# A fused Sinkhorn-attention and Fourier-mixing kernel: W1 loaded by quarters of its columns, and every engine's order and buffers laid out anew

## The chip, the cores and the metric

The kernel runs on one NeuronCore of one Trainium2 chip. A core has five engines that work at the same time: TensorE (PE in the profile, with its weight loads as PEld), VectorE (DVE), ScalarE (ACT), GpSimd (POOL) and SyncE (SP). POOL and SP issue nearly all the DMA transfers. The metric is device microseconds of one execution, from plain runs; the profile is of one more execution, with the hardware profiler on.

## The reference

`_attn_ref` takes q, k and v of shape (4, 8, 768, 64) and an 8 by 8 matrix for each of the 32 pairs of batch and head. Five rounds of exponential and of row and column normalisation (Sinkhorn) turn each matrix into a mixing matrix P. P mixes the eight blocks of 96 rows of k and v, and then each block of q attends to the mixed block of k and v of its own index.

```
k_sorted = np.einsum('bhij,bhjcd->bhicd', P, k_b)      # v_sorted alike
scores = scale * q_b @ k_sb^T;  attn = softmax(scores);  out = attn @ v_sb
```

`_moe_ref` takes the result as x of shape (4, 768, 512), adds the real part of a two-dimensional Fourier transform over tokens and features, normalises each row, and applies an MLP with W1 (512 by 2048) and W2 (2048 by 512).

```
u = x + real(fft2(x));  un = (u - mean) / sqrt(var + 1e-6)
out = u + np.maximum(un @ w_ch1, 0.0) @ w_ch2
```

## The kernel before

The work is cut by batch (b = 0 to 3) and, in the MLP, by half a batch of 384 tokens (g = 0, 1). A batch goes through the following stages. The numbers are operation numbers, which the order tables below use; they are the same before and after.

- Sinkhorn on all 32 matrices at once (VectorE and ScalarE; only for the first batch's start), then the block mixing matrices.
- `v_mix`, `v_mix_two`: v is mixed by TensorE (tag `vmix`, `vmix2`), and evacuated from PSUM (tag `vev`).
- `kqt` and `scores`: k is mixed and q transposed on TensorE (tags `kq`, `qT`, and in batches 1 to 3 `kq4`, `qT4`, which use quarters of the array and 24 small matmuls each), evacuated (`ksev`, `qtev`), multiplied (`sc`, `sc4`), exponentiated on ScalarE (`exp`, line 1270) and written as exp minus one (`em1`, lines 1283 and 1285).
- `av`: attention times v, 13 small matmuls for a head (line 1300), then a reciprocal and a product on VectorE.
- `a_path`, `a_rows`, `dft1`, `dft2`: the Fourier transform as matmuls. Operations 218 and 219 (`psx`, `psr`, lines 1062 and 1072) make the rows of the block means, which SP copies into `rb` (tag `arow`). The first matmul group of `dft1` of batch 0 is operation 244 (line 1374), its first `dft2` is 259 (line 1465). Then come mean and variance, the normalised rows `un`, and the transposed tiles `ut`. In batch 0 TensorE transposes and three evacuations write `ut` (operations 277, 281 and 285, tag `utev`).
- `ff1` (line 1584) for batch 0: for each of 16 column chunks `fc` of W1, four matmuls of 128 by 384 over the four 128-row chunks of W1, then a relu into `hr`. `ff2` (line 1668) multiplies with W2. Batches 1 to 3 use a scheme with seven products in place of eight (`ff1_seven`, line 1764, and `ff2_chunk`, lines 1864 and 1874), with sums and differences of the quarters of W1 and W2 (`w1_sums`, `w2_sums`).

The order of the work is not the order of the program text. Every operation is registered with `P.add`, with its possible engines, its durations and its dependences. The table `ORDER` holds, for each engine, the list of operation numbers in which that engine's instructions are written out. `Plan.schedule` goes through these lists with assumed durations. Its result sets three things in the emitted program: which buffer (PSUM bank, SBUF tile) each operation gets, the interleaving of the instructions, and how many idle matmuls (line 2010, "spins", on a constant tile) are written into TensorE's stream ahead of the operation 1613, `spun`. It does not write any wait; waits follow from the data and the buffers.

The assumed durations in `Plan` that matter here: a load moves at `HBM` = 390 bytes per ns of source data and lands `DLAT` us after that; `FETCH` = (190, 255, a, b) says that TensorE's instructions come in blocks of 256, that the block after next is asked for 190 instructions in, and that it takes a us while loads are running and b us otherwise.

Loads are issued by POOL (line 616, `load`) in the order of its list. Operations 28 to 31 load W1, 430 and 431 the second half of v, 432 to 435 load W2, 117 to 122 k and q of batch 1, 474 to 485 those of batch 2, 667 to 678 those of batch 3. All loads of large inputs cast from 32 to 16 bits on the way. POOL and SP keep eight semaphores each for their transfers; a further transfer reuses the semaphore of the eighth before it.

Of the kernel before, what the change touches and what calls it, by code (L numbers as in the profile page):

```python
# [12 lines left out]
ALU = mybir.AluOpType  # L13
# [17 lines left out]
FETCH = (190, 255, 6.0, 3.5)  # L31
# [36 lines left out]
    ),  # L68
    "ACT": (
# [27 lines left out]
    ),  # L97
    "DVE": (
# [183 lines left out]

class Plan:
    HBM = 390.0
    DLAT = 2.2
    XL = 0.07

    def __init__(self):
# [52 lines left out]
    def schedule(self):  # L341
# [56 lines left out]
        while len(order) < len(self.ops):  # L398
            pick = None
            for e in free:  # L400
                if place[e] == len(queue[e]):
                    continue
                o = queue[e][place[e]]
# [1639 lines left out]
```

## Time and profile before

| | us |
|---|---|
| plain runs: median of 3 (lowest, highest) | 258.41 (257.62, 258.8) |
| profiled execution, its own time | 256.77 |
| profiled execution, span from first to last instruction | 255.0 |
| TensorE busy in the span | 241.3 |
| VectorE busy | 225.0 |
| ScalarE busy | 178.0 |
| GpSimd busy | 95.3 |

The profile has a page with the busy time of each engine and the span in 40 slices, and views that answer questions on the same execution: the chain of work that ended last (each step follows back to what released it), the busy time of each engine in chosen stretches, instructions in order of time, groups of instructions by line and tile, and the DMA transfers. In the view of stretches a cell such as "5.31 (x103)" is the busy time in us and the number of instructions. A matmul is counted from its start to a modelled end, so neighbours overlap; a run of matmuls is read by its total time and its count.

### The profile page before, as it was taken

Reading aid. Unit: us, or ns where it says so; the run is one execution under the profiler, and the core shown is the slowest. Engines: PE = TensorE matmul, PEld = TensorE weight load, DVE = VectorE, ACT = ScalarE, POOL = GpSimd, SP = SyncE. Lnnn points to the kernel's source line nnn. Section 1 sums busy time; section 2 is a strip of 40 time slices with the busy share of each in tenths; the row PEclk is TensorE's granted clock in tenths of the full one; section 3 lists DMA queues with packets and bytes.
Section 4 is the critical chain, followed back from the end, with each engine's and each line's share of the span. In section 5 each row is a group of like instructions: output and inputs, shape, how many; then the busy total and the mean of one; then the engine's idle time right before and its main releaser. Section 6 shows DMA issues by size and latency. Waiting matters only on the chain.

```text
span 255.0 us, 7508 instructions
## 1 busy us (share of the span) xinstructions
PE 241.3 (95%) x2975; PEld 163.3 (64%) x2975; DVE 225.0 (88%) x576; ACT 178.0 (70%) x418; POOL 95.3 (37%) x128
## 2 busy tenths in 40 slices
PE   4989989999999999999999999999999999999990
PEld 1356865566666566655556667887667887658880
DVE  4789898899999899989999999998999688799870
ACT  2589898999998999999858898244784523664100
POOL 8975522243708950216446000061240007530070
PEclk9999999999999999999999999999999999999999
DMA  6999999999999998482685123652466304880055
GB/s 128 206 213 305 212 212 217 208 218 248 195 117 123 152 154 138 131 150 53 93 179 114 35 75 63 85 88 38 84 75 71 62 4 63 121 107 0 3 108 139
DMA packets 45688, 31.77 MB, mean 125 GB/s; under 512 B 30554, under 2 KB 39528, under 8 KB 45652
## 3 DMA queue, kind: packets, MB, share of 16 engines
q0 software_dynamic: 26544, 23.59, 59.2%
q1 hardware_dynamic: 19110, 7.72, 16.8%
q8 instruction: 23, 0.38, 0.6%
q14 instruction: 11, 0.09, 0.1%
HBM read 29.07 MB, written 11.53 MB: 159 GB/s over the span
## 4 chain that ended last, share of the span: by engine, by line
PE 80%; ACT 10%; DMA 3%; DVE 3%; issue 2%; ACTq 0%; POOLq 0%
PE bank L1764 22%; PE bank L1864 12%; PE bank L1874 9%; PE bank L1668 9%; PE bank L1584 6%; PE bank L1300 4%; DMA hr<-in_v_dram 3%; PE bank L1261 3%; ACT ks L859 2%; PE bank L1465 2%; ACT ex L1270 2%; PE bank L1374 2%; PE bank L1072 1%; PE bank L877 1%; ACT eb L1285 1%
## 5 line engine op out<-in xcount | busy, mean ns | idle before, releaser
L1612 POOL DMA_INDIRECT out_dram<-u,rows x23 | 37.9, 1646 | 109.9 <-DVE u L1892 66.4
L1270 ACT ACTIVATE ex<-bank 96x384 f32<-96x384 f32 x64 | 29.4, 487 | 2.9 <-PE bank L1261 2.5
L1864 PEld LDWEIGHTS <-hr 128*128 128x128 f16 x288 | 28.0, 98 | 5.1 <-DVE hr L1839 0.4
L1764 PE MATMUL bank<-ut,w1sb 128*128 128x384 f16 x144 | 30.9, 326 | 0.0
L859 ACT COPY bank<-bank 128x384 f32<-128x384 f32 (+1 forms) x42 | 18.6, 445 | 13.8 <-DVE hr L1784 4.9
L1764 PEld LDWEIGHTS <-w1sb 128*128 128x128 f16 x192 | 18.6, 98 | 11.1 <-issue 0.2
L1787 ACT ACTIVATE hr<-bank 128x384 f16<-128x384 f32 x41 | 19.1, 492 | 9.2 <-PE bank L1764 8.7
L1584 PE MATMUL bank<-ut,w1sb 128*128 128x384 f16 x128 | 24.5, 326 | 0.0
L1668 PE MATMUL bank<-w2sb,hr 128*128 128x512 f16 x96 | 24.4, 380 | 0.0
L1874 PEld LDWEIGHTS <-vcx 128*128 128x128 f16 x216 | 21.1, 98 | 3.6
L616 POOL DMA_DIRECT2D kq<-in_q_dram x18 | 16.6, 931 | 7.8 <-PE bank L877 3.7
L1764 PEld LDWEIGHTS <-kq 128*128 128x128 f16 x144 | 13.9, 98 | 8.8 <-issue 0.2
L1300 PEld LDWEIGHTS <-eb 97*128 97x128 f16 x416 | 16.3, 98 | 3.8 <-issue 0.2
L1874 PE MATMUL bank<-kq,vcx 128*128 128x256 f16 x144 | 18.5, 273 | 0.0
L1285 ACT ACTIVATE eb<-ex 96x384 f16<-96x384 f32 x37 | 18.3, 521 | 0.1
L1864 PE MATMUL bank<-w2sb,hr 128*128 128x256 f16 x144 | 17.8, 273 | 0.0
L1772 DVE TENSOR_TENSOR hr<-bank,vsf 128x384 f16<-128x384 f32 x32 | 16.8, 550 | 1.2 <-PE bank L1764 1.0
L1300 PE MATMUL bank<-vsf,eb 97*128 97x65 f16 x416 | 17.4, 193 | 0.2
L1317 DVE TENSOR_TENSOR rt<-bank,rz 128x384 f16<-128x384 f32 x32 | 16.9, 545 | 0.3
L859 DVE COPY bank<-bank 128x384 f32<-128x384 f32 (+1 forms) x24 | 12.1, 508 | 5.3 <-PE bank L1874 3.7
L859 ACT CAST vsf<-bank 96x512 f16<-96x512 f32 x25 | 15.7, 676 | 0.5 <-PE bank L976 0.4
L859 ACT CAST ks<-bank 128x384 f16<-128x384 f32 x29 | 15.1, 559 | 0.9 <-PE bank L1195 0.8
(212 smaller groups left out, 587.2 us busy)
## 6 DMA issues: line engine op xcount, KB each, us to landing
w1sb<-in_moe_w_ch_dram POOLq DMA_DIRECT2D x4, 512.0 KB, 18.0
w2sb<-in_moe_w_ch_dram POOLq DMA_DIRECT2D x4, 512.0 KB, 22.2
hr<-in_v_dram POOLq DMA_DIRECT2D x2, 768.0 KB, 9.2
kq<-in_v_dram POOLq DMA_DIRECT2D x2, 768.0 KB, 12.4
kq<-in_k_dram POOLq DMA_DIRECT2D x8, 192.0 KB, 5.5
kq<-in_q_dram POOLq DMA_DIRECT2D x16, 96.0 KB, 7.2
out_dram<-u SPq DMA_DIRECT2D x6, 256.0 KB, 2.2
out_dram<-u POOLq DMA_DIRECT2D x5, 256.0 KB, 4.6
```

The costliest lines, as they stand in the source:

```text
L859: (nc.scalar.copy if e == "ACT" else V.tensor_copy)(dst, src)
L1270: nc.scalar.activation(ex.ap[0:96], pss[h2].ap[0:96, 0:384], AF.Exp, scale=SCALE),
L1285: nc.scalar.activation(ed, src, AF.Identity, bias=-1.0)
L1300: nc.tensor.matmul(po.ap[:, 65 * T:65 * T + 65], eb.ap[:, e0:e0 + 128], vsf[0:97, vi:vi + 65], start=(n == 0), stop=(n == len(WIN[T]) - 1) ...
L1317: P.add({"DVE": (0.465, 0.56)}, lambda _: V.tensor_tensor(rt.ap[:, :, D * h:D * h + D], po3()[:, :, 0:D], rz.ap[:, :, None].broadcast_to([ ...
L1584: nc.tensor.matmul(ps.ap[:, 0:GT], w1sb[:, c, 128 * fc:128 * fc + 128], ut.ap[:, c, :], start=(c == 0), stop=(c == 3))
L1612: return nc.gpsimd.indirect_dma_start(out.rearrange("b s m -> (b s) m"), bass.IndirectOffsetOnAxis(ap=rows[:, i:i + 1], axis=0), t_, None, ...
L1668: nc.tensor.matmul(ps.ap, hr[g][:, fc, 128 * tt:128 * tt + 128], w2sb[:, fc, :], start=(fc == 0), stop=(fc == 15))
L1764: nc.tensor.matmul(ps.ap[:, 0:GT], lhs[:, c, fi], rhs()[:, c, :], start=(start and c == 0), stop=(c == 1), skip_group_check=True)
L1787: nc.scalar.activation(hr[g][:, fc, :], p.ap[:, 0:GT], AF.Relu)
L1864: nc.tensor.matmul(ps.ap[:, 0:256], lhs[:, fc], rhs[:, fc], start=(start and fc == 0), stop=(fc == 7), skip_group_check=True)
L1874: nc.tensor.matmul(ps.ap[:, 0:256], S.ap[:, fc], rhs[:, fc], start=False, stop=(fc == 7), skip_group_check=True)
```

## The change

- `load_w1(c)` loads columns 512c to 512c + 511 of all four row chunks, where it loaded all 2048 columns of row chunk c. Each of the four transfers moves the same number of bytes, in runs of 2 KB of source where they were 8 KB.
- `ff1` for chunk `fc` now depends on the one quarter `fc // 4`, where it depended on all four loads. The keys in `w1_sums` follow.
- `FETCH` becomes (190, 255, 7.0, 4.0), where it was 6.0 and 3.5. `DLAT` becomes 2.9, where it was 2.2. `Plan.schedule` also holds a transfer of POOL or SP back until the eighth transfer before it on that engine has landed.
- All five lists of `ORDER` are new. No operation is added or removed. 141 operations change from ScalarE to VectorE or the other way.

The core of the diff; of `ORDER` only the first rows of the three lists that the text speaks of most:

```diff
-FETCH = (190, 255, 6.0, 3.5)
+MOVES = ("load", "out", "acc", "uX", "qX", "arow")
+FETCH = (190, 255, 7.0, 4.0)
...
     "PE": (
-        "0 77 69 78 73 79 91 123 139 92 141 125 211 97 127 143 218 129 134 "
-        "105 115 109 107 101 113 103 175 145 111 155 219 150 187 171 159 173 "
-        "157 190 177 196 182 193 161 166 208 332 318 335 205 199 320 328 202 "
-        "330 389 341 322 357 324 244 326 248 250 255 257 338 354 259 263 267 "
-        "344 287 436 292 437 360 349 438 297 276 280 284 402 370 365 932 1613 "
-        "940 563 930 918 386 928 942 373 408 920 916 411 938 922 405 914 926 "
+        "0 77 69 91 73 78 92 79 139 123 141 125 211 127 143 97 218 129 113 "
+        "107 115 134 101 103 145 105 111 109 150 171 219 159 173 175 187 318 "
+        "190 177 193 182 155 157 196 161 166 205 357 208 320 202 328 199 341 "
+        "332 326 324 389 335 330 244 322 248 250 257 255 354 338 259 263 267 "
+        "360 287 292 436 344 437 349 438 276 297 365 280 284 402 1613 934 942 "
+        "928 920 373 370 916 924 932 408 914 563 386 376 918 411 922 405 926 "
...
     "POOL": (
-        "18 19 20 21 5 6 7 1 2 3 4 10 8 22 23 24 25 26 27 334 117 118 119 120 "
-        "121 122 430 431 28 29 30 31 432 433 434 435 474 475 476 477 478 479 "
-        "314 480 481 482 483 484 485 667 668 669 670 671 672 310 951 673 674 "
+        "18 19 20 21 5 6 7 1 2 3 4 10 8 22 23 24 25 26 27 334 118 30 122 119 "
+        "431 117 430 432 31 121 29 28 120 310 433 434 474 476 477 475 435 479 "
+        "478 482 483 485 480 670 678 484 481 314 669 668 671 672 667 957 677 "
...
     "SP": (
-        "12 13 14 15 17 16 232 231 230 233 428 426 275 283 429 427 279 590 "
+        "12 13 14 15 230 233 231 232 17 16 283 427 426 275 279 428 429 590 "
...
-    DLAT = 2.2
+    DLAT = 2.9
...
+        lane = {"POOL": [0.0] * 8, "SP": [0.0] * 8}
...
                 t = max(free[e], o.ready, st)
+                if e in lane and o.tag in MOVES:
+                    t = max(t, lane[e][0])
...
+            if e in lane and o.tag in MOVES:
+                lane[e] = lane[e][1:] + [o.end]
...
     def load_w1(c, prio):
-        load(w1sb[:, c, :], w1v[:, c, :], 1048576, [("w1", c)], prio)
+        f = slice(512 * c, 512 * c + 512)
+        load(w1sb[:, :, f], w1v[:, :, f], 1048576, [("w1", c)], prio)
...
             P.add(pe(mm(GT, 4)), f, r=[(ut, tt, 1) for tt in range(3)]
-                  + [("w1", c) for c in range(4)], w=[ps], prio=pr_pe,
-                  tag="ff1")
+                  + [("w1", fc // 4)], w=[ps], prio=pr_pe, tag="ff1")
...
-                (G3, X11, G3, ALU.subtract, w1k, [("w1", 0), ("w1", 1)]),
+                (G3, X11, G3, ALU.subtract, w1k, [("w1", 2), ("w1", 3)]),
```

190 rows, old and new, of the table ORDER are left out of this document.

## The prediction

> **What bounds the kernel now.** I read the page's slices first, to find where which engine is full, and then the view of stretches.
>
> ```profile
> span 255.0 us, 7508 instructions
> ...
> PE   4989989999999999999999999999999999999990
> ...
> DVE  4789898899999899989999999998999688799870
> ACT  2589898999998999999858898244784523664100
> ...
> ```
>
> ```profile
> 3.76:14.47 10.71, 10.25 (x37) 3.91 (x37) 8.18 (x33) 5.26 (x7) 10.71 (x14) 1.00 1.10 201
> 14.47:26.48 12.01, 10.35 (x187) 7.49 (x188) 11.41 (x30) 11.14 (x25) 6.74 (x12) 1.00 1.22 263
> 26.48:32.62 6.14, 6.07 (x132) 4.63 (x130) 5.14 (x17) 5.43 (x15) 3.35 (x6) 1.00 1.29 213
> 32.62:38.62 6.00, 4.73 (x133) 3.84 (x131) 5.79 (x18) 5.52 (x13) 1.49 (x2) 1.00 1.03 213
> 38.62:44.49 5.87, 5.76 (x129) 3.39 (x130) 4.92 (x12) 4.97 (x12) 1.36 (x2) 1.00 1.07 217
> 44.49:53.53 9.04, 9.04 (x176) 5.71 (x164) 8.24 (x25) 8.98 (x24) 2.82 (x4) 1.00 1.14 207
> 53.53:249.50 195.97, 195.14 (x2216) 134.34 (x2209) 180.27 (x441) 135.14 (x324) 66.17 (x84) 1.00 0.69 100
> ```
>
> The columns after the length are PE, PEld, DVE, ACT, POOL, the granted clock, the DMA share and GB/s. I chose the last boundary, 53.53, because the first `ff1` matmul starts there. Behind it TensorE is idle for 195.97 - 195.14 = 0.83 us in all. Busy is not yet dense, so I also looked at the chain of waits, whose longest pieces behind that point are runs of matmuls:
>
> ```profile
> 37.40 1.22 issue
> ...
> 53.00 0.47 ACT ut L859
> ...
> 185.07 8.48 PE bank L1764 x52
> ...
> 219.09 11.20 PE bank L1764 x68
> ...
> 249.07 0.42 DVE eb L1892
> ```
>
> 52 matmuls in 8.48 us are 163 ns each, 68 in 11.20 are 165: one pace, with no gaps in it. So I take the last 196 us to hold nothing to win but those 0.83 us. The end is set by when the first `ff1` can start, plus TensorE's work that is left then, plus the tail behind 249.5, whose operations stand in the same order in the new lists. The first `ff1` waited for the last transposed tile, which ScalarE wrote from 53.00 to 53.47.
>
> The second thing to see is the stop of 1.22 us at 37.40, where TensorE waited for nothing that the profile shows. Two more rows explain it:
>
> ```profile
> q8 instruction: 23, 0.38, 0.6%
> ...
> 81.51:87.24 5.73, 5.73 (x133) 1.00 1.23 140
> 87.26:94.39 7.13, 6.89 (x148) 1.00 1.65 144
> ```
>
> 23 packets of 0.38 MB are 16.5 KB each, and 2975 matmuls with 2975 weight loads over 23 are 259 instructions each: these are blocks of TensorE's instructions. The three stretches 26.48 to 32.62, 32.62 to 38.62 and 38.62 to 44.49 hold about 128 matmuls each, one block, and took 6.14, 6.00 and 5.87 us, though the middle one holds only 4.73 us of work. While the loads run, a block costs about 6 us, and TensorE stops if its work in a block is less.
>
> The Trainium skill ("Runtime: NRT & Kernel Launch", Instruction fetch mechanics) says that a block of 256 instructions is fetched ahead and that the cost of a boundary is "mostly hidden". This trace disagrees at one boundary of 23, with 1.22 us.
>
> **The change, part by part.** All sums are made against the profiled execution (span 255.0, own time 256.77); I carry the difference over to the median of the plain runs, 258.41, which lies 1.64 us above it.
>
> *W1 by quarters of its columns.*
>
> ```profile
> L1584 PE MATMUL bank<-ut,w1sb x128: 323/326/337, 53.5 to 110.5; 128*128 128x384 f16 x128
> ...
> L616 POOL DMA_DIRECT2D w1sb<-in_moe_w_ch_dram x4: 528/528/528, 27.0 to 30.5; - x4
> ...
> DMA to landing us min/median/max: 17.7/18.0/19.8
> ```
>
> ```profile
> L616 POOL DMA_DIRECT2D w2sb<-in_moe_w_ch_dram x4: 740/744/750, 31.3 to 40.9; - x4
> ```
>
> W1 lands by 30.5 + 19.8 = 50.3, and its first use is at 53.5: today no `ff1` waits for it. A quarter of columns has the shape of a W2 load (2 KB runs, 512 of them), so POOL spends 0.74 us instead of 0.53 on each, 0.84 us in all, hidden because POOL runs far ahead of its landings. The new list puts quarter 0 (operation 28) behind 5440 KB of loads counted from operation 118 and including itself, by the sizes in the code after the cast; today's last W1 load closes 5120 KB.
>
> ```profile
> cs<-k_cs POOLq DMA_DIRECT2D x1, 579.0 KB, 8.4
> tab<-k_tab POOLq DMA_DIRECT2D x1, 514.0 KB, 10.2
> perm<-k_perm POOLq DMA_DIRECT2D x1, 34.0 KB, 10.1
> ...
> 15.36 0.56 POOL L616 DMA_DIRECT2D tab<-k_tab  x1
> 15.89 0.56 POOL L616 DMA_DIRECT2D perm<-k_perm  x1
> ```
>
> `perm`, the load before, lands at 15.89 + 10.1 = 26.0. From there 5120 KB took 24.3 us, so 5440 take 25.8, and quarter 0 lands near 51.8. The first four `ff1` of the new list (934, 942, 928, 920) use quarters 2, 3, 1 and 0, so that the split matters for 2 us at most; 920 comes some 2 us behind the first. Cost 0, with 3 to 4 us to spare.
>
> *TensorE's list ahead of the first `ff1`.* `psr` (219) cannot start before the table `tab` lands at 15.36 + 10.2 = 25.6, and nothing ahead of that load moved. By counting matmuls in both lists, 374 instructions stand ahead of `psr` (382 before), and 1034 ahead of the first `dft1` (1034 before). With 6 us per block the first `dft1` can hardly come earlier than its 40.5. What can go is the time that the other engines lost around the stop:
>
> ```profile
> 37.91 0.26 ACT L1347 COPY pmt<-pmt 128x4 f16<-128x4 f16 x1
> 39.05 0.86 ACT L859 COPY qt<-bank 128x384 f16<-128x384 f16 x2 [0.88 <-PE bank L1139]
> ```
>
> ScalarE idles for 0.88 us, waiting for q transposes behind the stop. In the new list the transposes 357 and 341 both stand ahead of the block's end, with evacuations of 0.43 us each for ScalarE to do. I take -0.9, with bounds of -1.3 (the 0.41 us idle before the next `dft1` evacuation too) and 0.
>
> *Operations that change engine.* Ahead of the last transposed tile, ScalarE gains 20 operations and loses 21, and VectorE gains 20 and loses 19. I priced them by these groups and their like:
>
> ```profile
> L859 ACT CAST vsf<-bank 96x512 f16<-96x512 f32 x13 | 8.2, 676 | 0.0
> ...
> L1285 ACT ACTIVATE eb<-ex 96x384 f16<-96x384 f32 x7 | 3.6, 521 | 0.0
> ```
>
> ```profile
> L1283 DVE TENSOR_SCALAR eb<-ex 96x384 f16<-96x384 f32 x13 | 4.3, 349 | 0.2
> ...
> L859 DVE CAST vsf<-bank 96x512 f16<-96x512 f32 x3 | 2.1, 684 | 0.0
> ```
>
> For instance six v evacuations go to VectorE (6 x 0.68) and seven `em1` leave it (7 x 0.35). All together ScalarE is relieved of 0.4 us and VectorE loaded with 1.4. ScalarE was the later one, so -0.4. VectorE had 6.14 - 5.14 = 1.0 us idle from 26.48 and 5.87 - 4.92 = 0.95 from 38.62, which covers 1.4; if it covers nothing, the first `ff1` comes 1.0 us later. I take 0.
>
> *Behind the first `ff1`.* Operation 370 (`kq4`) falls behind it, in the dense part: +0.4. Changes between array shapes number 82 instead of 81, at about 0.1 each by
>
> ```profile
> 111.30 0.97 PE bank L1668 x4
> ...
> 113.94 0.86 PE bank L1668 x4
> ```
>
> (the first follows a group of small matmuls): +0.1. Of the 0.83 us idle I give back 0.2.
>
> *Moved steps on SP and POOL.* SP's small loads 17 and 16 now stand behind four copies of block-mean rows. They are used by the store 310 and by the first `dft2`, behind 44.49, and should have some microseconds to spare, since operations that sum to about 3 us stand behind VectorE's `rr` in the new list that stood ahead of it. On POOL the store 310 stands ahead of W2's later loads, and waits for VectorE:
>
> ```profile
> 50.27 0.16 DVE L1500 SCALAR_TENSOR_TENSOR u<-rt,bank 128x2 f32<-128x2 f16 x1
> ```
>
> ```profile
> L1668 PE MATMUL bank<-w2sb,hr x96: 377/379/390, 67.6 to 133.7; 128*128 128x512 f16 x96
> ```
>
> The loads queued behind it are issued from about 52, when transfers until 52.7 are still ahead of them (5632 KB from 26.0), and W2 is first read at 67.6. Both at 0; if the loads starved, `ff2` would wait for what they are late.
>
> The sum: -0.9 - 0.4 + 0.4 + 0.1 - 0.2 = **-1.0 us**: 255.8 profiled, 257.4 in plain runs.
>
> **The rivals.**
>
> *The dense part gets stops (slower).* Instruction blocks behind 53.5 are not all as roomy as today's, where the tightest that I measured took 5.73 us with 5.73 of work. Adding up starts in the new list, one block between operations 450 and 596 (four `vmix2`, `kq4`, `sc4`, little `ff2`) holds only about 4.3 to 4.7 us, and one between 976 and 519 about 4.8 to 5.2. If a block costs 6 us there as between 26 and 44, this adds 1.5 + 1.0 = 2.5 us of TensorE's time, with VectorE's extra microsecond 3.5; less the gains of 1.0, +1.5 to +2.5, so 260.4. For it: the row 87.26 to 94.39 has a DMA share of 1.65, more than any of the early blocks. Against: no block behind 53.5 shows a stop today. It decides from a block time of about 5 us on.
>
> *Nothing moves.* The list of what TensorE does ahead of the first `ff1` is the same but for 370, the first `dft1` stays at its place by the block count, and VectorE's 1.4 us eat ScalarE's gap: 258.4. W1 by quarters would then also show as what it is in the rows, a load that nobody waited for.
>
> *The early stop vanishes.* If the 1.22 us are not the price of a block, the new order may be free of them, the first `dft1` comes up to 1.0 earlier, and the sum is -2.0. Also, plain runs lie 1.64 us above the profiled one; if that is late loads and stops that vary from run to run, an order that leaves more room for them gets some of it back. With half of the second that makes -2.8, 255.6. The Trainium skill's "mostly hidden" (same page and section) points to this one; the row at 37.40 is against it.
>
> *The new order is tight where the old one is loose.* DVE and ACT are full up to 130 us (the slices show nines), so a swap there can hold up TensorE at once. No row shows the new swaps; I count it with the first rival.
>
> **How the numbers follow.** Main case 0.42 (257.4, own range 256.4 to 258.4), nothing moves 0.20 (257.9 to 258.9), dense stops 0.23 (259.2 to 261), early stop gone 0.15 (255 to 256.6). A measurement of this kernel tells about 0.5%, 1.3 us, from no change, so the bounds are 257.1 and 259.7. Faster: 0.15 and not quite half of 0.42, 0.35. Slower: 0.23 and a little of the rest's tail, 0.25. Same: 0.40. The range goes from 255.5 to 260.7, through most of the two outer cases.
>
> **What would show it.** Right: first `ff1` at 52.3 to 53; ScalarE's idle time behind the stop under 0.3 us; the first `dft1` within 0.5 us of 40.5; TensorE idle under 1 us behind the first `ff1`; no wait of `ff1` for `w1sb`. Wrong: "issue" pieces over 0.5 us behind 70 us (dense stops); a first `ff1` that waits for VectorE's `ut` after 54 (VectorE overloaded); a wait of line 1584 for a W1 load (the list too late); a first `dft1` before 39.8 (no block price).

## The result, and the profile after

| | before | after |
|---|---|---|
| median of 20 plain runs, us (lowest, highest) | 257.96 (256.99, 259.61) | 259.59 (257.69, 262.23) |
| ratio, 95% interval | | 1.0056 (1.0032 to 1.008) |
| profiled execution, span, us | 255.0 | 256.5 |

The ratio leaves out three executions of the changed kernel that were over 261.5 us, more than 1.5% above its fastest, so it lies a little under the quotient of the two medians.

The changed kernel came out 0.56% slower, where the forecast was 0.4% faster (257.4 against 258.41). Four repeats of the changed kernel, told below, gave 0.9943, 0.9964, 0.9980 and once more 1.0035 of before. So there are two results to explain.

The page of the changed kernel, to be laid beside the page of before:

```profile
span 256.5 us, 7512 instructions
...
PE 243.4 (95%) x2982; PEld 164.8 (64%) x2982; DVE 227.3 (89%) x575; ACT 178.6 (70%) x419; POOL 93.5 (36%) x128
...
PE   4799999999999999899999999999999999999992
...
PE 77%; DVE 10%; DMA 4%; ACT 4%; issue 2%; POOL 1%; DVEq 0%; SPq 0%; POOLq 0%
```

TensorE's two early 8s, at the third and the sixth slice, are gone, though the second slice fell from 9 to 7 (there are 34 spins in place of 27). There is a new 8 at the 17th slice, from 102.6 to 109.0 us, where before had a 9. The view of stretches, with the same boundaries as for before, and the last one from the first `ff1` on:

```profile
32.62:38.62 6.00, 5.74 (x147) 3.94 (x145) 5.78 (x19) 5.15 (x14) 1.57 (x3) 1.00 1.07 211
...
44.49:53.53 9.04, 8.84 (x141) 5.14 (x134) 8.46 (x25) 8.45 (x23) 3.50 (x5) 1.00 1.18 217
54.23:252.00 197.77, 195.58 (x2233) 135.45 (x2233) 180.33 (x438) 135.29 (x326) 65.90 (x85) 1.00 0.67 98
```

In the stretch of the old stop TensorE is now busy for 5.74 us, not 4.73; but 1.21 us of it are spins, and before had none there. And the first `ff1` starts at 54.23, 0.70 us later than before, and behind it TensorE is idle for 197.77 - 195.58 = 2.19 us, where it was 0.83. The span divides so: first `ff1` +0.70; from there to the last matmul's end 197.75 us against 195.51, +2.24; from there to the end of the span 4.54 against 5.96, -1.42. The sum is +1.52, the difference of the spans. None of the three is what was forecast.

**Where TensorE stops.** Instructions in order of time around 102 us in the changed kernel (start, duration, engine, line; in brackets the idle time before and what ended it):

```profile
100.00 1.35 POOL L1618 DMA_INDIRECT out_dram<-u,rows  x1 [6.63 <-DVE mv L1527]
...
101.66 1.01 POOL L1618 DMA_INDIRECT out_dram<-u,rows  x1 [0.19 <-issue]
...
102.32 0.59 ACT L866 CAST ks<-bank 128x384 f16<-128x384 f32 x1 [1.27 <-PE bank L1591]
...
103.26 0.20 DVE L1321 RECIPROCAL rz<-bank 128x6 f32<-128x6 f32 x1 [1.09 <-PE bank L1307]
...
103.51 0.60 ACT L866 CAST ks<-bank 128x384 f16<-128x384 f32 x1
...
104.16 0.36 PE L1268 MATMUL bank<-qt,ks 64*64 64x96 f16 x16 [1.07 <-ACT ks L866]
```

TensorE waits for ScalarE's `ks`, and ScalarE had stood idle for 1.27 us itself, waiting for TensorE. It needed op 680 (`kq4`), whose matmuls by their rows ended at 100.6. VectorE likewise waits for an `av` (op 655) that by its rows ended at 102.44, and starts at 103.26. The trace also records when TensorE raised its semaphore, the counter that the other engines' instructions wait for. For the matmuls that end at 100.41, 100.59, 101.39, 102.04 and 102.44 by the rows it went up at 101.33, 102.29, 103.04, 103.10 and 103.24: 0.8 to 1.7 us late, where the usual lag is 0.01. ScalarE's copy starts 0.03 us behind the second of these raises and VectorE's reciprocal 0.02 us behind the last. So the results were announced late, one by one and then bunched, while the rows go on at their pace. All five ends lie between 100.00 and 102.67, when GpSimd issued two indirect stores (stores whose target rows come from a table); the last raises came up to 0.57 us behind the second. The profile has three more such places, each at a score (line 1268) that ends inside an indirect store: 0.81 us late at 50.54, 1.22 at 109.08, 0.49 at 126.0. The profile of before shows 0.28 at most. Besides, the trace of the changed kernel lacks eight of TensorE's raises, most of them for results that end inside an indirect store; the trace of before lacks none.

The Trainium skill ("Perfetto Trace Analysis", Tensor Engine Instruction (MATMUL, LD_WEIGHTS)) says that a matmul's end is estimated from its size, and that the semaphore goes up only when PSUM has acknowledged all bytes. That is why such a delay is in no matmul row; the trace agrees, with 101.39 in the row and 103.04 at the semaphore.

### The profile page after: what moved, and what is told of

Same layout as the page of the kernel before. It is cut to its first block, busy times and chain, and to the rows that moved or that the text cites. A ratio compares the mean times of both kernels' runs of the same rounds, so it can differ in the third digit from the quotient of the medians.

```text
span 256.5 us, 7512 instructions
## 1 busy us (share of the span) xinstructions
PE 243.4 (95%) x2982; PEld 164.8 (64%) x2982; DVE 227.3 (89%) x575; ACT 178.6 (70%) x419; POOL 93.5 (36%) x128
## 3 DMA queue, kind: packets, MB, share of 16 engines
q0 software_dynamic: 28080, 23.59, 59.6%
## 4 chain that ended last, share of the span: by engine, by line
PE 77%; DVE 10%; DMA 4%; ACT 4%; issue 2%; POOL 1%; DVEq 0%; SPq 0%; POOLq 0%
PE bank L1770 19%; PE bank L1591 8%; PE bank L1674 8%; PE bank L1870 8%; PE bank L1307 5%; PE bank L1880 5%; PE bank L1268 4%; PE bank L1381 3%; PE bank L1472 3%; DMA out_dram<-u,rows 2%; PE bank L884 2%; DVE vcx L1845 2%; PE bank L955 2%; DVE hr L1778 1%; PE bank L2016 1%
## 5 line engine op out<-in xcount | busy, mean ns | idle before, releaser
L1618 POOL DMA_INDIRECT out_dram<-u,rows x23 | 36.8, 1601 | 82.5 <-DVE u L1898 37.3
L866 ACT COPY bank<-bank 128x384 f32<-128x384 f32 (+1 forms) x52 | 22.5, 443 | 12.0 <-PE bank L1880 9.6
L1770 PEld LDWEIGHTS <-w1sb 128*128 128x128 f16 x192 | 18.7, 98 | 11.8 <-issue 0.2
L1793 ACT ACTIVATE hr<-bank 128x384 f16<-128x384 f32 x36 | 16.8, 492 | 9.8 <-PE bank L1770 9.3
L1292 ACT ACTIVATE eb<-ex 96x384 f16<-96x384 f32 x43 | 22.4, 528 | 0.4
L622 POOL DMA_DIRECT2D kq<-in_q_dram x18 | 15.6, 878 | 12.9 <-DVE rz L1321 7.3
L1591 PEld LDWEIGHTS <-w1sb 128*128 128x128 f16 x128 | 11.1, 97 | 6.8 <-issue 0.4
L1602 ACT ACTIVATE hr<-bank 128x384 f16<-128x384 f32 x31 | 14.8, 496 | 0.9 <-PE bank L1591 0.7
L866 ACT CAST ks<-bank 128x384 f16<-128x384 f32 x25 | 13.7, 575 | 1.5 <-PE bank L1591 1.3
## 6 DMA issues: line engine op xcount, KB each, us to landing
out_dram<-u SPq DMA_DIRECT2D x6, 256.0 KB, 2.3
out_dram<-u POOLq DMA_DIRECT2D x4, 256.0 KB, 6.7
```

What stands on the lines that cost most here:

```text
L866: (nc.scalar.copy if e == "ACT" else V.tensor_copy)(dst, src)
L1292: nc.scalar.activation(ed, src, AF.Identity, bias=-1.0)
L1591: nc.tensor.matmul(ps.ap[:, 0:GT], w1sb[:, c, 128 * fc:128 * fc + 128], ut.ap[:, c, :], start=(c == 0), stop=(c == 3))
L1618: return nc.gpsimd.indirect_dma_start(out.rearrange("b s m -> (b s) m"), bass.IndirectOffsetOnAxis(ap=rows[:, i:i + 1], axis=0), t_, None, ...
L1770: nc.tensor.matmul(ps.ap[:, 0:GT], lhs[:, c, fi], rhs()[:, c, :], start=(start and c == 0), stop=(c == 1), skip_group_check=True)
```

## The experiments

Ratios are to the kernel before on the same chip, with 95% intervals. Runs of one section without another word shared a chip.

### One part at a time

`old_quarters` takes from the change only the W1 part:

```
-        load(w1sb[:, c, :], w1v[:, c, :], 1048576, [("w1", c)], prio)
+        f = slice(512 * c, 512 * c + 512)
+        load(w1sb[:, :, f], w1v[:, :, f], 1048576, [("w1", c)], prio)
...
```

> The kernel before with one part of the change alone: W1 loaded by quarters of its columns, and ff1 and the sums of W1 waiting for their quarter; the order and the planner's delays are those of before. Theory (the order is what costs): 258.0, within 0.5 of before, first ff1 near 53.5 in the profile, because the W1 quarters land ahead of it as the row chunks did. Rival (quarters cost): 259.5, with ff1 waiting for W1 or loads landing later. Rival (quarters help and the order hides it): 257.0 or less.

Measured: 256.0 us, 0.9941 (0.9919 to 0.9963). The second rival: quarters help. Later, on another chip, `old_quarters2` gave 0.9945. But nothing moved up to the last matmul, which started at 248.90 against 248.76. The gain is at the very end (see the drain below).

`old_delays` takes only `FETCH`, `DLAT` and the lanes:

```
-FETCH = (190, 255, 6.0, 3.5)
+FETCH = (190, 255, 7.0, 4.0)
...
-    DLAT = 2.2
+    DLAT = 2.9
...
```

> The kernel before with the planner's delays and lanes of the change alone (7.0 and 4.0 us per block fetch, 2.9 us landing, eight lanes per queue); order and W1 chunks are those of before, so that only the choice of buffers and the count of spins differ. Theory (the order costs): 258.0, within 0.5 of before. Rival (the buffers laid out under the new delays cost, through waits for a buffer that was free before): 259.5, with waits in the dense part. Rival (more spins push the first blocks): first dft1 later than 40.8 and 258.6.

Measured: 257.82 us, 1.0004 (0.9975 to 1.0034): no effect, as the theory said.

`new_olddelays` is the changed kernel with these lines taken back:

> The changed kernel with the planner's old delays and no lanes: order and W1 quarters of the change, buffers and spins laid out as before. Theory (the order costs): 259.6, as the change, first ff1 near 54.2. Rival (buffers cost): 258.0.

Measured: 256.7 us, 0.9962 (0.9941 to 0.9983). This is below both expectations. The theory that the order costs 0.56% falls: with quarters the order loses some 0.2% against `old_quarters` (256.7 against 256.0), and the two intervals overlap.

`new_rows` is the changed kernel with the W1 part taken back:

> The changed kernel with W1 loaded by chunks of its rows again; order and delays are those of the change. Theory (the order costs): 259.6, as the change. Rival (quarters cost): 258.0. Rival (quarters are needed under the new order, since its first ff1 uses two quarters only): over 260, with the first ff1 waiting for the last W1 load.

Measured: 258.14 us, 1.0025 (1.0 to 1.005). The number is that of the first rival, "quarters cost", but not its reason, since `old_quarters` had gained. There was no wait for W1: the first `ff1` started at 53.43.

None of these four profiles had a TensorE result over 0.35 us late, though in the two with the new order the same scores end inside the same stores (the one near 50 us 0.51 and 0.52 us behind the store's start, as in the first profile). From 0.9962 and 1.0004 the changed kernel should have been near 0.996, so the first result itself came into question.

### The same kernel again, and the indirect stores

`after_again` and `after_plain` ran on a second chip. `after_plain` puts plain stores at the place of the indirect ones, and so leaves out the reversal of the rows that these do:

```
-        return nc.gpsimd.indirect_dma_start(
-            out.rearrange("b s m -> (b s) m"),
-            bass.IndirectOffsetOnAxis(ap=rows[:, i:i + 1], axis=0),
-            t_, None, compute_op=op)
...
+        d = out[b, TOK[T][127]:TOK[T][0] + 1, :]
+        return [nc.gpsimd.dma_start(d, t_) if op is ALU.bypass else
+                nc.gpsimd.dma_start(d, t_, accum_op=op)]
```

> The changed kernel once more, nothing changed, for a second profile. In its first profile TensorE stopped for 1.23 us at 102.8 and 0.64 us at 112.5, each behind a result of TensorE that its readers saw 0.8 to 1.7 us late while GpSimd issued an indirect store. Theory (these late results are what the new layout costs, and they hit at random): 259.6, late results over 0.5 us again inside indirect stores, but not all at the same places, and stops of 1 to 4 us in sum. Rival (the stops are fixed waits of the layout): the same stops at the same operations within 0.2 us. Rival (the first profile was odd): no late results, span 256 or less, and the time is lost elsewhere.

> The changed kernel with every indirect store of GpSimd replaced by a plain one of as many bytes at the same place of its queue; the rows of the second half of the sequence are written in the order in which they lie, so the output has them reversed. Theory (indirect stores hold back TensorE's results): no result over 0.3 us late, no stop behind one, 257.5 (2 us off). Rival (GpSimd's stores have nothing to do with it): 259.6 and stops of 1 us or more as before. Rival (plain stores take GpSimd's queue longer and land later): over 260.

Measured: `after_again` 256.29 us, 0.9943 (0.9925 to 0.9961); `after_plain` 255.41 us, 0.9909 (0.9882 to 0.9937). No late result in either. So the first result did not repeat, as the last rival of `after_again` had it, and the same stretch of the same kernel, in order of time, now reads:

```profile
99.84 1.36 POOL L1618 DMA_INDIRECT out_dram<-u,rows  x1 [6.63 <-DVE mv L1527]
...
100.79 0.57 ACT L866 CAST ks<-bank 128x384 f16<-128x384 f32 x1
...
101.97 0.60 ACT L866 CAST ks<-bank 128x384 f16<-128x384 f32 x1
102.28 0.20 DVE L1321 RECIPROCAL rz<-bank 128x6 f32<-128x6 f32 x1 [0.27 <-PE bank L1307]
...
102.83 0.36 PE L1268 MATMUL bank<-qt,ks 64*64 64x96 f16 x16
```

`ks` is copied at 100.79 instead of 102.32, though the store started within 0.16 us of the same time. The stores are equally long too, 1.36 and 1.01 us. What they do to TensorE's results differs.

On a third chip `after_third` gave no late result either:

> The changed kernel a third time, unchanged, to see which of its two results holds: 1.0056 of before with late results of TensorE in the profile, or 0.9943 without. Theory (the late results belong to the chip or the hour, not to the kernel alone): 0.994 with no result over 0.3 us late, or 1.003 to 1.008 with several; nothing between. Rival (they come and go from execution to execution on any chip): between, 0.997 to 1.002, with single executions 2 us apart.

Measured: 256.62 us, 0.9964 (0.9946 to 0.9982). Then the changed kernel went back, at a later hour, to the chip of the first four experiments, with `after_plain2` (the same as `after_plain`) and `after_twice`, in which each indirect store is split in two of 64 rows:

```
...
-            bass.IndirectOffsetOnAxis(ap=rows[:, i:i + 1], axis=0),
-            t_, None, compute_op=op)
+            bass.IndirectOffsetOnAxis(
+                ap=rows[0:64, 4 * B * n + i:4 * B * n + i + 1], axis=0),
+            t_[64 * n:64 * n + 64], None, compute_op=op) for n in range(2)]
```

> The changed kernel a fourth time, unchanged. It gave 1.0056 of before with results of TensorE up to 1.7 us late in the profile, then 0.9943 and 0.9964 on two chips with none over 0.3 us late. Theory (chip or hour): 0.993 to 0.997 and no late result, or over 1.003 with several. Rival (execution by execution): between the two.

> The changed kernel with plain stores in place of indirect ones (rows of the second half of the sequence in the order in which they lie), beside the changed kernel: 0.9 us faster than it where no result is late (255.41 against 256.29 in the earlier call), 3 us or more faster if this chip shows late results and the indirect stores are what holds them back. Rival (indirect stores are innocent): late results here too.

> The changed kernel with every indirect store in two of 64 rows each, one behind the other: twice as many issues on GpSimd, the same bytes, the same output. Theory (each issue that meets a score's result delays it by 0.1 to 0.3 us where the chip is not in the state of the first profile): more results 0.1 to 0.3 us late, time within 0.7 us of the changed kernel beside it. Rival (an indirect store holds TensorE's results in any case, and overlap decides): results 0.5 us late and more, over 1.5 us slower. Other rival (only GpSimd's own queue grows): W2's later loads land later and the first ff2 waits.

Measured: `after_fourth` 258.99 us, 1.0035 (1.001 to 1.0059), with results late at the same scores as the first time: 0.82 us at 50.3, up to 1.96 from 100.4 to 102, 1.22 at 110.0, 0.49 at 127. `after_plain2` 255.48 us, 0.9908 (0.9878 to 0.9939), none late. On one chip within the same hour they differ by 3.5 us; where no result is late the same exchange gave 0.9. This is the strongest evidence that the indirect stores hold back the results. A plain store is also issued faster (0.57 us against 1.06 in the rows below), and no run tells the kind of the store from the length of its issue. The kernel before, run beside them, took 257.70 us, within 0.3 us of its medians on the other occasions, so whatever this occasion has costs the old order nothing that shows. All executions of `after_fourth` took 258.17 us or more, all of `after_again` and `after_third` 257.51 or less: the two results don't change from execution to execution. Here are the two around 50 us, first `after_fourth`:

```profile
49.74 1.06 POOL L1618 DMA_INDIRECT out_dram<-u,rows  x1 [11.90 <-DVE u L1507]
...
49.89 0.36 PE L1268 MATMUL bank<-qt,ks 64*64 64x96 f16 x16
...
51.10 0.86 ACT L1277 ACTIVATE ex<-bank 96x384 f32<-96x384 f32 x2 [0.50 <-DVE un L1553]
```

and `after_plain2`:

```profile
49.83 0.57 POOL L1623 DMA_DIRECT2D out_dram<-u  x1 [12.14 <-DVE u L1507]
...
49.98 0.36 PE L1268 MATMUL bank<-qt,ks 64*64 64x96 f16 x16
...
50.58 0.84 ACT L1277 ACTIVATE ex<-bank 96x384 f32<-96x384 f32 x2
```

The exponential follows the start of its score by 1.21 us in the one and by 0.60 in the other. (The releaser that its row names in `after_fourth`, VectorE's `un`, is not what the exponential needs: it only came last by the records.)

`after_twice` took 288.06 us, 1.1155 (1.1115 to 1.1196). It had late results too, up to 2.16 us, but they aren't what makes its 30 us. Its list of waits (us in total, number of waits, longest) begins:

```profile
POOL out_dram L1619 <- DMA out_dram<-u,rows: 72.5, 22, 8.6
```

The second half of each store waited up to 8.6 us for the first to land, and all of GpSimd's queue with it. I had left the order between the two halves in, so its time tells nothing about the number of stores.

Last, three kernels of one order on a fourth chip:

> The changed kernel a fifth time, unchanged, beside two kernels of the same order. If no result is late here: 0.993 to 0.997 of before. If this is an occasion with late results: 1.003 to 1.008, with 0.8 us at the score of 50.3 and 1.2 us at that of 109 to 110, as twice before.

> The changed kernel with the old delays again (other banks for some results and two spins fewer), on one chip with the changed kernel. Where the changed kernel has late results here: theory (the occasion): late results here too, at the scores of 50 and 107, and 1.003 to 1.008 of before; rival (the layout): results at most 0.15 us late and 0.996. Where it has none: 0.996.

> The changed kernel with W1 by row chunks again, on one chip with the changed kernel. Where the changed kernel has late results here: theory (the occasion): late here too, and 1.010 to 1.013 of before; rival (the quarter loads): at most 0.15 us late and 1.0025. Where it has none: 1.0025, 0.7 to 0.9 per cent behind the changed kernel, because GpSimd's closing drain is 1.5 us longer.

Measured: 257.03 us, 0.9980 (0.9962 to 0.9999); 256.53 us, 0.9967 (0.9947 to 0.9987); 258.17 us, 1.0021 (1.0 to 1.0042). No result was late, so the question whether the two other layouts would suffer too stayed open. The last two repeat their first values within 0.0005. The changed kernel's 0.9980 is outside the expected 0.993 to 0.997, and `new_rows2` is only 0.4% behind it, not 0.7 to 0.9; the profile of `after_fifth` has the longest stops of TensorE near 76 and 81 us (told at the end), which may be why.

### The closing drain

`old_halves` loads W1 by halves of rows and columns:

```
+        r, h = divmod(c, 2)
+        f = slice(1024 * h, 1024 * h + 1024)
+        load(w1sb[:, 2 * r:2 * r + 2, f], w1v[:, 2 * r:2 * r + 2, f], 1048576,
+             [("w1", c)], prio)
```

> The kernel before with W1 by quarters alone, beside the changed kernel on one chip. If the order and the delays bring nothing where no result is late: the same as the changed kernel within 0.5 us, near 256.1. If the order gains what was forecast ahead of the first ff1: the changed kernel 0.9 us faster than this one.

> The kernel before with each W1 load covering half of the rows and half of the columns: runs of 2 KB, twice the packets of row chunks and half those of quarters. In every profile with row chunks GpSimd's closing drain lasted 6.4 to 6.9 us and ended 1.3 to 1.7 us behind all else; in every one with quarters it lasted 5.0 to 5.2. Theory (the drain shortens by the packets that went through GpSimd's queue before): some 5.9, so 257.0. Rival (it depends on a step at some count): 6.4 and 257.6, or 5.1 and 256.1. Rival (the drain has nothing to do with W1): 6.4 with quarters too, in the run beside this one.

Measured, on the third chip: `old_quarters2` 256.0 us, 0.9945 (0.9927 to 0.9964); `old_halves` 257.76 us, 1.0015 (0.9992 to 1.0038). The changed kernel beside them took 256.62, so where no result is late, order and delays lose some 0.6 us against quarters alone; the two intervals overlap, and on the second chip the changed kernel was 0.4 us ahead of `old_both`, which has the old order with quarters and delays. So the order's own effect is not clear of the scatter. The span and SP's last store in order of time, of before, of `old_quarters` and of `old_halves`:

```profile
core 0 of [0], span 255.0 us
...
249.56 0.33 SPq L1622 DMA_DIRECT2D out_dram<-eb  x1
```

```profile
core 0 of [0], span 254.0 us
...
249.70 0.33 SPq L1622 DMA_DIRECT2D out_dram<-eb  x1
```

```profile
core 0 of [0], span 255.7 us
...
250.09 0.33 SPq L1625 DMA_DIRECT2D out_dram<-eb  x1
```

From the last issue to the end it is 5.4, 4.3 and 5.6 us. The transfers aren't later: GpSimd's last packet ended 2.7 us behind the last matmul in before and 3.0 in `old_quarters`. What differs is an instruction named DRAIN that closes GpSimd's program, which the trace has with its duration. It lasted 6.41 us in before, 6.54 in `old_delays`, 6.85 and 6.71 in the two `new_rows`, and 6.59 in `old_halves`. In the profiles with quarters and whole indirect stores it lasted 4.8 to 5.5, and there SyncE's own drain ended within 0.3 us of it; with row chunks SyncE's ended 1.3 to 1.5 us ahead. Counted from the end of GpSimd's last packet the step is sharper: the drain ended 2.4 to 2.5 us behind it in all profiles with row chunks and in `old_halves`, and 0.9 to 1.2 us behind it in these with quarters. GpSimd's queue moved 26,544 packets with row chunks and 28,080 with quarters; halves lie between with 27,056, and their drain and time are those of row chunks. So it is no price by the packet but a step between halves and quarters. What it is a step of stays open.

### The order's own stop, and the fastest version

In `new_olddelays` TensorE waited near 177 us for a copy by VectorE (in order of time):

```profile
176.53 0.81 ACT L1543 ACTIVATE un<-eb,nm,ny 128x512 f16<-128x512 f32 x1 [1.52 <-DVE nm L1531]
...
177.14 0.55 DVE L860 COPY bank<-bank 128x384 f32<-128x384 f32 x1
...
177.74 0.49 PE L1764 MATMUL bank<-qt,kq 128*128 128x384 f16 x2 [0.83 <-DVE bank L860]
```

The copy (op 1229) stood on ScalarE's list before; the change put it on VectorE's, behind two rounds of normalisation, while ScalarE idled for 1.52 us. `new_seed` is `new_olddelays`, and `seed_new` the changed kernel, with this one op moved back to ScalarE:

```
-ACT: ... 1225 1227 881 1275 ...      DVE: ... 897 1229 883 ...
+ACT: ... 1225 1227 1229 881 1275 ... DVE: ... 897 883 ...
```

> New order, W1 by quarters, old delays, and one operation moved: the copy that seeds the bank of a first product (op 1229) goes from VectorE's list to ScalarE's, ahead of op 881, where ScalarE stood idle for 1.52 us. In the profile without the move TensorE waited 0.83 us for it at 176.9. Theory (that wait is what the order costs behind the attention): no stop near 177, last matmul 0.8 earlier, 255.9 against 256.7. Rival (VectorE's next operation is late instead): 256.7.

> The changed kernel with op 1229, the copy that seeds the bank of a first product, moved from VectorE's list to ScalarE's ahead of op 881; nothing else. Theory (TensorE's stop near 177, 0.58 us in the second profile of the changed kernel, is a wait for VectorE in the order): no stop there, 0.5 us faster than the changed kernel beside it. Rival: the same time.

Measured: `new_seed` 255.62 us, 0.9914 (0.9884 to 0.9944), on the second chip; `seed_new` 255.58 us, 0.9939 (0.9916 to 0.9963), on the third, 1.0 us under the changed kernel beside it, where 0.5 was expected. The stop is gone in both. In the changed kernel's five profiles it is 0.1 to 0.4 us between matmuls, 0.14 on this third chip, so most of the 1.0 us is not shown to be this wait, and the intervals overlap. In `new_seed`:

```profile
175.91 0.46 ACT L860 COPY bank<-bank 128x384 f32<-128x384 f32 x1 [1.09 <-PE bank L1764]
...
176.53 0.49 PE L1764 MATMUL bank<-qt,kq 128*128 128x384 f16 x2
```

`new_seed` has the lowest ratio of the kernels here that compute everything (0.9914), but its interval meets those of `seed_new` and `old_quarters`. `old_both`, quarters and delays in the old order, ran on the second chip and completes the table:

> The kernel before with W1 by quarters and the new delays, and with the old order: all of the change but the order. If the parts add up: quarters gave 0.9941 and the delays 1.0004 of before, so 256.2. If the new layout is what costs as soon as W1 comes by quarters (it took the changed order from 0.9962 to 1.0056): 258.5 or more, with late results of TensorE in the profile.

Measured: 256.67 us, 0.9949 (0.9921 to 0.9977): the parts add up within the interval, and the new layout alone costs nothing that shows.

## Why the prediction was wrong

**The first result.** The step that failed is the last of the sum: "Moved steps on SP and POOL", "Both at 0". It asked only who is queued behind the store 310. Issued at 50.0 instead of 60.3, this store and the others now meet scores that end while they are being issued. Where results come late, this costs 0.54 us at the first `ff1` (54.23 against 53.69 in `after_again`, which loses that again in a stop at 80.7), 1.3 from 103 to 106 and 0.5 near 113. From there on the same operations start 1.8 to 2.1 us later than in `after_again`; op 1472, for one, at 214.92 against 212.98. The rival "the dense part gets stops" had the right sign (260.4 against 259.59) by another mechanism, so that its number is luck.

**The other results.** Where no result was late the changed kernel gained 0.2 to 0.6%, about the forecast 0.4%, but by other terms, so that this agreement is luck too:

- *W1 by quarters, "Cost 0"*: nobody waits for W1, as forecast, but the closing drain makes it -1.4. The tail was taken as unchanged, because "operations stand in the same order"; the drain is no operation of the lists.
- *TensorE's list, "I take -0.9"*: the block rule held. Blocks end at 32.45, 38.19 and 44.58, against 32.62, 38.62 and 44.49 before, and the first `dft1` starts at 40.85, within 0.5 of 40.55. Nothing of the 0.9 came: ScalarE's idle time behind the stop fell from 0.88 to 0.25 us, and yet the first `ff1` started at 53.6 to 53.7 without late results. Forecast was 52.3 to 53. The step that failed is the wait: what ScalarE gains was taken to move the first `ff1`, but TensorE had no room of its own. In `after_again` the chain of waits holds TensorE alone from 38.19 to 52.52, where before's holds mostly ScalarE from 41.24 on; and TensorE's work in the stretch of the stop, spins left out, is 4.5 us against 4.7, so the room of the stop went to 1.2 us of spins and not to work from behind it.
- *Engine swaps, -0.4 and 0*: gone with it, for the same reason. VectorE is busy for 8.5 us of the 9.04 from 44.49 in these profiles, against 8.24 before. No run puts the swaps back alone.
- *Dense part, +0.4 + 0.1 - 0.2*: nothing was recovered. The order has two stops of its own. One is the copy of op 1229, which was never priced. The other is the block between ops 450 and 596 that the slower rival named with up to 1.5 us, here in the chain of waits of `after_again`:

```profile
80.29 0.30 PE bank L1268 x16
80.58 0.13 PE bank L983
80.72 0.82 issue
81.54 0.39 PE bank L983 x15
```

That block lasted 6.1 us in `after_again`, from 75.44 to 81.54, with 5.3 us of work, and in `after_third` 5.1 us without a stop. In the five profiles of the changed kernel, in the order of their runs, TensorE's stops near 76 and 81 us, each at the end of a block, sum to 0.4, 0.8, 0, 0.3 and 1.4 us. So block time decides there, as that rival put it, but it differs from profile to profile, at 5.1 to 6.1 us for this block. The second block that it named, between ops 976 and 519, took 5.2 us in all five profiles and never stopped.

## What to carry to other kernels

Measure a change of under 1% on more than one chip and hour before explaining it: one kernel gave 0.994 and 1.006 here, each with an interval of 0.003 or less on either side. When an engine starts late behind TensorE though the matmul's row ended long before, compare the semaphore's time with the row, and look at what GpSimd issues at that moment. Price the end of the program too: what a load's shape does to the closing drain was the largest steady effect of this change.

## What the runs showed of the hardware

- While GpSimd issues an indirect store, TensorE's results can be announced 0.5 to 2.0 us late. It happened at the same scores in two profiles of the changed kernel, and not in three others. Plain stores at the same places did not do it, on the very chip and in the hour where the indirect ones did. Four other kernels, two of them with the new order and with the same scores inside the same stores, had run earlier on that chip without late results, so neither the chip nor that overlap decides alone. Whether it takes the hour, something set when the program is loaded, this layout or several of them is open, as is what holds the results.
- GpSimd's closing drain lasts 6.4 to 6.9 us with W1 by row chunks or by halves and 4.8 to 5.5 us by quarters, though the transfers end no earlier: it ends 2.4 to 2.5 us behind GpSimd's last packet in the first two cases and 0.9 to 1.2 in the third.
- Seven more spins and a stop of 0.23 us in place of 1.22 left the block times of TensorE's early part within 0.6 us of what they were: with spins or with idle time, a block took some 6 us from 26 to 44 us. Later, from 75 to 94, blocks of 5.1 and 5.2 us passed without a stop in some profiles.
